# Other column cuts in the last output tile, and another queue for its second store

## The chip, the cores and the metric

The kernel runs on one core of a Trainium2 chip. The metric is the device time of one execution in microseconds; three runs of the kernel before gave a median of 223.0 us (222.99 to 223.22). One further execution was taken by the hardware profiler. Engines are named as in the profile: PE is TensorE's matmuls and PEld its weight loads, DVE is VectorE, ACT is ScalarE, POOL is GpSimd, SP is SyncE, which issues most of the DMAs. "SPq" and "ACTq" in a row stand for a DMA issued by SP or ACT.

## What is computed

The input is x, 2048 tokens of 640 columns in bf16. With xn the layer norm of x over its columns, the output is `x + s * g`:

- s is a linear attention with 32 heads of 20 columns: q, k and v come from `xn @ wqkv`; q and k go through `where(t > 0, t + 1, exp(t)) + 1e-6`; per head the sums over all tokens of k times v and of k alone are formed; q times the first is divided by q times the second, and the result goes through `wo`.
- g is `silu(relu(xn @ w1) @ w2)` with 1728 hidden columns.

```
s = _A_ref(xn, A_wqkv, A_wo)
g = _silu(_B_ref(xn, B_w1, B_w2))
return x + s * g
```

## The kernel before, in words

The tokens are cut into 16 tiles of 128. A first part of the kernel normalizes, makes k and its feature map for every tile, q for every block of 512 tokens (`pqT`) and the hidden layer (`hT`). A middle part forms the sums over the tokens, divides q by its denominator in place (`pqT`), and folds v's weights, the sums and `wo` into one matrix `wf` of 640 x 640, so that s of a tile is just `pqT` of that tile times `wf`. The last part makes the output tile by tile.

In that last part the tiles are taken in 8 pairs, `pairs[p]`; the last pair is tiles 11 and 15. For a tile, `U_main` (line 841) and `U_halves` (line 857) make the second matmul of g into two banks of PSUM, 320 columns in each; `U_silu` (lines 872 and 875) is the Silu on ACT into `g_sb`; `s_tile` (line 879) makes s and the output. `bank(p, u)` (line 834) says which two of the eight PSUM banks a tile uses; `HN` is 320 and `D` is 640.

`s_tile` for any tile but the last: ten matmuls (line 887), five for each half of 320 columns, since the sum runs over 640 rows in 5 chunks of 128; then one product on DVE, s from PSUM times g, into a buffer `tmpo` (line 909); one addition on DVE, `tmpo` plus x, into `outb` (line 894); one DMA to the output, issued by SP (line 897).

`s_tile` for the last tile, tile 15 (call on line 967, `last=True`): the columns are cut into three parts (line 885), each with five matmuls into a bank of its own: columns 0 to 319, 320 to 511 and 512 to 639. DVE makes one product for each (line 902). After the first product POOL adds x to the first part (line 906) and SP stores it; the second and third part get one addition on DVE over 320 columns (line 907) and one store, issued by SP as well. The helper `add` (line 893) holds the addition and its store.

Who waits for whom is not written by hand: a small scheduler (`Sched`) keeps, for each named piece of a buffer, its last writer and readers, and puts a wait on a semaphore ahead of an instruction where one is needed. Every engine runs its own list strictly in the order in which the program names the operations. A product of the last tile names both halves of g, `gk` (lines 891 and 904), so each waits for both Silu instructions of the tile; the second of these (line 962) works on columns 320 to 639. A DMA stands in the list of the engine that issues it, takes a semaphore of its own and counts as landed when that has reached 16. At the end SP waits for all DMAs (line 969), and a barrier over the engines closes the program (line 971).

ACT issues one DMA in the whole kernel before, a piece of w1 at the very start (line 369); all others are SP's.

Of the kernel before, what the change touches and what calls it, by code (L numbers as in the profile page):

```python
# [211 lines left out]
def bass_recurrent_scan__linear_attn_block__dense_activation_relu__prompt_kernel(  # L212
# [9 lines left out]
    Bb, S, D = A_x.shape  # L222
# [11 lines left out]
    HN = D // 2  # L234
# [11 lines left out]
    out2 = out[0]  # L246
# [17 lines left out]
    outb = reg3[:, VC * D:(VC + NOUT) * D].rearrange("p (a n) -> p a n", a=NOUT)  # L264
# [48 lines left out]
    def ps2(b, n):  # L313
        return psT[:, 512 * b:512 * (b + 2)].rearrange("p (a n) -> p a n", a=2)[:, :, 0:n]
# [7 lines left out]
    def dma(E, fn, R=(), W=(), extra=()):  # L322
        i = nds[0]
        nds[0] += 1
        return sc.dma(E, fn, i, R=R, W=W, extra=extra)

    def tok(t):
        return slice(P * t, P * (t + 1))
# [155 lines left out]
    def two(ap):  # L484
        return ap.rearrange("p (a n) -> p a n", a=2)
# [219 lines left out]
    for j in range(1, J):  # L705
# [11 lines left out]
        for n, (kind, jj, f) in enumerate(blocks):  # L717
# [4 lines left out]
            if j + 1 < J:  # L722
# [6 lines left out]
                if n in (9, 12, 14, 17):  # L729
                    t = t0 + (9, 12, 14, 17).index(n)  # L730
# [103 lines left out]
    def bank(p, u):  # L834
        return 4 * ((p + 1) % 2) + 2 * u
# [43 lines left out]
    def s_tile(p, u, b, last=False):  # L879
        t = pairs[p][u]  # L880
        os_ = so[0] % NOUT
        so[0] += 1
        i = t // 4

        parts = [(b, 0, HN), (b + 1, HN, 512), (bank(7, 0), 512, D)] if last else [(b, 0, HN), (b + 1, HN, D)]
        for pb, lo, hi in parts:
            sc.group("PE", [(lambda eng, c=c, pb=pb, lo=lo, hi=hi: eng.matmul(  # L887
                ps[pb][:, 0:hi - lo], lhsT=pqT[:, c, tok(t)], rhs=wf[:, c, lo:hi],
                start=(c == 0), stop=(c == C - 1))) for c in range(C)],
                R=[("pqT", i, c) for c in range(C)] + wfk, W=[("ps", pb)])  # L890
        gk = [("g", t, 0), ("g", t, 1)]

        def add(E, lo, hi, keys):
            sc.op(E, lambda eng: eng.tensor_tensor(out=outb[:, os_, lo:hi], in0=tmpo[:, os_, lo:hi],  # L894
                                                   in1=xre[:, t, lo:hi], op=ALU.add),
                  R=[("tmpo", os_, k) for k in keys] + [("xre", t // 4)], W=[("outb", os_, k) for k in keys])
            dma("SP", lambda eng: eng.dma_start(out2[tok(t), lo:hi], outb[:, os_, lo:hi]),
                R=[("outb", os_, k) for k in keys])

        if last:  # L900
            for k, (pb, lo, hi) in enumerate(parts):
                sc.op("DVE", lambda eng, pb=pb, lo=lo, hi=hi: eng.tensor_tensor(  # L902
                    out=tmpo[:, os_, lo:hi], in0=ps[pb][:, 0:hi - lo], in1=g_sb[:, t, lo:hi], op=ALU.mult),
                    R=[("ps", pb)] + gk, W=[("tmpo", os_, k)])
                if k == 0:
                    add("POOL", lo, hi, (0,))
            add("DVE", HN, D, (1, 2))
        else:
            sc.op("DVE", lambda eng: eng.tensor_tensor(  # L909
                out=two(tmpo[:, os_, :]), in0=ps2(b, HN), in1=two(g_sb[:, t, :]), op=ALU.mult),  # L910
                R=[("ps", b), ("ps", b + 1)] + gk, W=[("tmpo", os_, k) for k in range(3)])
            add("DVE", 0, D, (0, 1, 2))
# [31 lines left out]
    U_main(1, 1)  # L944
    U_silu(1, 1)
    s_tile(0, 0, 4)
    s_tile(0, 1, 6)
    for p in range(2, 8):
        opens = p % 2 == 1
        U_main(p, 0)  # L950
        if opens:
            U_silu(p, 0)
        s_tile(p - 1, 0, bank(p - 1, 0))
        U_main(p, 1, (0,))
        if p == 7:
            U_silu(p, 1, 0)
        s_tile(p - 1, 1, bank(p - 1, 1))
        if p == 7:
            s_tile(p, 0, bank(p - 1, 0))
        U_main(p, 1, (1,))  # L960
        if opens:
            U_silu(p, 1, 1 if p == 7 else None)
        else:
            U_halves((p, p + 1))
            U_silu(p, 0)
            U_silu(p, 1)
# [34 lines left out]
```

## Time and profile before

| what | value |
|---|---|
| median of 3 runs | 223.0 us (222.99 to 223.22) |
| the profiled execution's own time | 223.15 us |
| its span in the profile | 221.4 us |
| granted TensorE clock, mean | 0.999 |
| busy: PE, PEld, DVE, ACT, POOL (us) | 215.8, 133.9, 114.6, 86.1, 43.7 |
| stores to the output | 15 of 160 KB, 2 of 80 KB |

The span is the time from the first to the last instruction that the profile holds; the execution's own time is 1.75 us longer (223.15 less 221.4), which lies before and after. Times in rows are counted from the start of the span. A row of the timeline has the start, the duration, engine, line, operation, output and inputs with their shapes, and in brackets how long the engine was idle before and who ended that. Rows of equal instructions are merged ("x5"), and the duration is then from the first's start to the last's end. A DMA's row has the time that the issuing engine was busy with it; its landing is given apart, counted from the issue.

### The profile page before, as it was taken

Reading aid. Unit: us, or ns where it says so; the run is one execution under the profiler, and the core shown is the slowest. Engines: PE = TensorE matmul, PEld = TensorE weight load, DVE = VectorE, ACT = ScalarE, POOL = GpSimd, SP = SyncE. Lnnn points to the kernel's source line nnn. Section 1 sums busy time; section 2 is a strip of 40 time slices with the busy share of each in tenths; the row PEclk is TensorE's granted clock in tenths of the full one; section 3 lists DMA queues with packets and bytes.
Section 4 is the critical chain, followed back from the end, with each engine's and each line's share of the span. In section 5 each row is a group of like instructions: output and inputs, shape, how many; then the busy total and the mean of one; then the engine's idle time right before and its main releaser. Section 6 shows DMA issues by size and latency. Waiting matters only on the chain.

```text
span 221.4 us, 3528 instructions
## 1 busy us (share of the span) xinstructions
PE 215.8 (97%) x1463; PEld 133.9 (60%) x1474; DVE 114.6 (52%) x193; ACT 86.1 (39%) x138; POOL 43.7 (20%) x66
## 2 busy tenths in 40 slices
PE   7999999999999999999999999999999999999994
PEld 2865554455545554444467778767767776776672
DVE  2687845889687999996710006603322222314063
ACT  2368665567656656555322114641021102110300
POOL 4053101259222998700000000000000000000001
PEclk9999999999999999999999999999999999999999
DMA  6899581211012105800059969369110101000002
GB/s 190 242 357 250 131 234 41 59 30 33 0 30 59 33 0 104 170 12 3 0 178 365 272 178 353 93 201 322 62 59 3 61 30 33 30 31 33 30 30 89
DMA packets 28156, 24.51 MB, mean 111 GB/s; under 512 B 11796, under 2 KB 27500, under 8 KB 28140
## 3 DMA queue, kind: packets, MB, share of 16 engines
q1 hardware_dynamic: 27484, 23.79, 36.7%
q10 hardware_dynamic: 656, 0.49, 0.8%
q8 instruction: 11, 0.18, 0.4%
q14 instruction: 5, 0.04, 0.1%
HBM read 15.75 MB, written 5.24 MB: 95 GB/s over the span
## 4 chain that ended last, share of the span: by engine, by line
PE 95%; DVE 1%; DMA 1%; issue 0%; ACT 0%
PE psT L841 26%; PE psT L555 25%; PE psT L472 10%; PE psT L786 10%; PE psT L540 10%; PE psT L887 10%; DMA reg<-in_A_x_dram 1%; PE psT L857 1%; PE psT L577 1%; PE psT L797 1%; PE psT L808 1%; PE psT L645 1%; PE psT L450 1%; DVE reg L902 0%; DVE stats L392 0%
## 5 line engine op out<-in xcount | busy, mean ns | idle before, releaser
L555 PE MATMUL psT<-reg 128*128 128x512 bf16 (+1 forms) x295 | 59.8, 346 | 0.7 <-issue 0.2
L841 PE MATMUL psT<-reg,hT 128*128 128x320 bf16 x416 | 60.1, 299 | 0.0
L841 PEld LDWEIGHTS psT<-reg,hT 128*128 128x128 bf16 x416 | 40.4, 98 | 16.4 <-issue 1.1
L555 PEld LDWEIGHTS psT<-reg 128*128 128x128 bf16 x305 | 27.3, 98 | 26.8 <-issue 0.4
L909 DVE TENSOR_TENSOR reg<-psT,reg 128x640 bf16<-128x640 f32 x15 | 12.4, 825 | 54.0 <-PE psT L887 53.9
L562 ACT ACTIVATE hT<-psT 128x512 bf16<-128x512 f32 x52 | 30.9, 598 | 18.2 <-PE psT L555 18.1
L875 ACT ACTIVATE reg<-psT 128x640 bf16<-128x640 f32 (+1 forms) x13 | 8.4, 661 | 44.3 <-PE psT L841 24.9
L894 POOL TENSOR_TENSOR reg<-reg 128x320 bf16<-128x320 bf16 x1 | 0.8, 788 | 124.6 <-DVE reg L902 124.6
L540 PE MATMUL psT<-reg 128*128 128x512 bf16 x99 | 24.6, 379 | 0.1
L472 PE MATMUL psT<-reg 128*128 128x320 bf16 x160 | 24.2, 299 | 0.0
L481 POOL TENSOR_TENSOR zacc<-zacc,reg 128x640 f32<-128x640 f32 x16 | 23.7, 1484 | 1.9 <-DVE reg L515 1.0
L887 PE MATMUL psT<-reg,pqT 128*128 128x320 bf16 (+2 forms) x165 | 24.0, 295 | 0.0
L786 PE MATMUL psT<-reg 128*128 128x320 bf16 x160 | 21.9, 299 | 0.0
L472 PEld LDWEIGHTS psT<-reg 128*128 128x128 bf16 x160 | 15.6, 98 | 8.2
L887 PEld LDWEIGHTS psT<-reg,pqT 128*128 128x128 bf16 x165 | 15.9, 98 | 6.0
L786 PEld LDWEIGHTS psT<-reg 128*128 128x128 bf16 x160 | 15.7, 98 | 6.2
L550 DVE SCALAR_TENSOR_TENSOR pqT<-er 128x512 bf16<-128x512 bf16 x20 | 17.1, 853 | 0.7
L540 PEld LDWEIGHTS psT<-reg 128*128 128x128 bf16 x100 | 9.7, 98 | 11.7 <-DVE er L548 0.6
L392 DVE BATCH_NORM_STATS2 stats<-reg 128x6 f32<-128x320 bf16 x32 | 14.0, 478 | 3.4 <-DMA reg<-in_A_x_dram 3.4
L547 ACT ACTIVATE er<-psT 128x512 bf16<-128x512 f32 x20 | 12.0, 598 | 8.9 <-PE psT L540 8.1
L548 DVE TENSOR_SCALAR er<-psT 128x512 bf16<-128x512 f32 x20 | 13.6, 679 | 3.1 <-ACT er L547 3.1
L515 DVE TENSOR_TENSOR reg<-ek 128x640 bf16<-128x640 bf16 x16 | 13.5, 843 | 1.5 <-ACT ek L506 1.0
(66 smaller groups left out, 134.6 us busy)
## 6 DMA issues: line engine op xcount, KB each, us to landing
reg<-in_A_x_dram SPq DMA_DIRECT2D x16, 160.0 KB, 4.1
rscr<-rden SPq DMA_DIRECT2D x4, 640.0 KB, 10.7
reg<-rscr SPq DMA_DIRECT2D x5, 512.0 KB, 6.1
reg<-in_A_x_dram SPq DMA_DIRECT2D x4, 640.0 KB, 6.2
out_dram<-reg SPq DMA_DIRECT2D x15, 160.0 KB, 1.8
reg<-in_A_wqkv_dram SPq DMA_DIRECT2D x2, 800.0 KB, 6.9
reg<-in_B_w_dram SPq DMA_DIRECT2D x1, 1120.0 KB, 5.9
reg<-in_B_w_dram SPq DMA_DIRECT2D x1, 1040.0 KB, 7.6
```

The lines of the kernel that those rows point to most:

```text
L392: sc.op("DVE", lambda eng, a=a: eng.bn_stats(stats[:, t, a, :], xv[:, HN * a:HN * (a + 1)]), R=[("xin", t % XR)], W=[("stats", t, a)])
L472: fns.append(lambda eng, a=a, k=k: eng.matmul(ps[b + a][:, 0:HN], lhsT=xnT[:, k, tok(t)], rhs=wqk[:, k, D + HN * a:D + HN * (a + 1)], star ...
L481: sc.op("POOL", lambda eng: eng.tensor_tensor(out=zacc[:, :], in0=zacc[:, :], in1=pk[:, t, :], op=ALU.add), R=[("zacc",), ("pk", t)], W=[( ...
L515: sc.op("DVE", lambda eng: eng.tensor_tensor(out=pk[:, t, :], in0=e_, in1=r_, op=ALU.add), R=[("ek_e", es), ("ek_r", es)], W=[("pk", t)])
L540: sc.group("PE", [(lambda eng, k=k: eng.matmul(ps[b], lhsT=wqk[:, k, P * f:P * (f + 1)], rhs=rhs(k), start=(k == 0), stop=(k == C - 1))) f ...
L548: sc.op("DVE", lambda eng: eng.tensor_scalar(out=r_, in0=ps[b], scalar1=0.0, scalar2=1e-6, op0=ALU.max, op1=ALU.add), R=[("ps", b), ("er_e ...
L550: sc.op("DVE", lambda eng: eng.scalar_tensor_tensor(out=pqT[:, f, schunk(j)], in0=e_, scalar=1.0, in1=r_, op0=ALU.min, op1=ALU.add), R=[(" ...
L555: return sc.group("PE", [(lambda eng, k=k: eng.matmul(ps[b][:, lo:hi], lhsT=w1_sb[:, k, P * f:P * (f + 1)], rhs=xnT[:, k, 512 * j + lo:512 ...
L562: sc.op("ACT", lambda eng: eng.activation(out=hT[:, f, schunk(j)], in_=ps[b], func=ACTF.Relu), R=[("ps", b)], W=[("hT", j, f)])
L786: fns.append(lambda eng, t=t, a=a: eng.matmul(ps[b + a][:, 0:HN], lhsT=xn[:, t, P * k:P * (k + 1)], rhs=pk[:, t, HN * a:HN * (a + 1)], sta ...
L841: sc.group("PE", [(lambda eng, f=f, n=n: eng.matmul(ps[b + n][:, 0:HN], lhsT=hT[:, f, tok(t)], rhs=w2_sb[:, f, HN * n:HN * (n + 1)], start ...
L887: sc.group("PE", [(lambda eng, c=c, pb=pb, lo=lo, hi=hi: eng.matmul(ps[pb][:, 0:hi - lo], lhsT=pqT[:, c, tok(t)], rhs=wf[:, c, lo:hi], sta ...
```

## The change

The last tile is cut into 256, 192 and 192 columns in place of 320, 192 and 128. POOL's addition and the first store then cover 256 columns (64 KB) in place of 320 (80 KB), DVE's addition and the second store 384 columns (96 KB) in place of 320. And the second store is issued by ACT in place of SP: `add` gets a parameter for the issuing engine.

```diff
-        parts = [(b, 0, HN), (b + 1, HN, 512), (bank(7, 0), 512, D)] if last else [(b, 0, HN), (b + 1, HN, D)]
+        parts = [(b, 0, 256), (b + 1, 256, 448), (bank(7, 0), 448, D)] if last else [(b, 0, HN), (b + 1, HN, D)]
...
-        def add(E, lo, hi, keys):
+        def add(E, lo, hi, keys, Q="SP"):
...
-            dma("SP", lambda eng: eng.dma_start(out2[tok(t), lo:hi], outb[:, os_, lo:hi]),
+            dma(Q, lambda eng: eng.dma_start(out2[tok(t), lo:hi], outb[:, os_, lo:hi]),
                 R=[("outb", os_, k) for k in keys])
...
-            add("DVE", HN, D, (1, 2))
+            add("DVE", 256, D, (1, 2), "ACT")
```

## The prediction

> **What bounds the kernel now.** I read the page first, then the chain of work that ended last, then the timeline of the last 5 us, and then single rows for the durations.
>
> ```profile
> span 221.4 us, 3528 instructions
> PE 215.8 (97%) x1463; PEld 133.9 (60%) x1474; DVE 114.6 (52%) x193; ACT 86.1 (39%) x138; POOL 43.7 (20%) x66
> PE 95%; DVE 1%; DMA 1%; issue 0%; ACT 0%
> ```
>
> PE is the bound nearly everywhere: 97% busy, 95% of the chain. The change touches no matmul but those of the last tile, so only what lies behind the last other matmul can move. The chain's end, in order of time (start, duration, what):
>
> ```profile
> 215.00 1.77 PE psT L841 x13
> 216.76 0.69 PE psT L887 x5
> 217.45 0.02 issue
> 217.48 0.99 DVE reg L902 x3
> 218.47 0.02 issue
> 218.49 0.52 DVE reg L894
> ```
>
> The reader is to see that PE hands over at 217.45, with the first part of the last tile, and that the rest is DVE: three products, then one addition, done at 218.49 + 0.52 = 219.01. The view stops there, as the rest is DMA. The same stretch in the timeline:
>
> ```profile
> 216.46 1.49 PEld L887 LDWEIGHTS psT<-reg,pqT 128*128 128x128 bf16 x15
> 216.60 1.53 PE L887 MATMUL psT<-reg,pqT 128*128 128x320 bf16 x15
> 216.80 0.44 ACT L875 ACTIVATE reg<-psT 128x320 bf16<-128x320 f32 x1 [4.05 <-PE psT L841]
> 218.05 0.79 POOL L894 TENSOR_TENSOR reg<-reg 128x320 bf16<-128x320 bf16 x1 [124.64 <-DVE reg L902]
> 218.86 0.33 SPq L897 DMA_DIRECT2D out_dram<-reg  x1
> 219.24 0.43 SPq L897 DMA_DIRECT2D out_dram<-reg  x1
> ```
>
> PE's 15 matmuls end at 216.60 + 1.53 = 218.13. POOL's addition ends at 218.84 and SP issues the first store at 218.86. The second store could go at 219.01, when its addition is done, but SP is busy with the first until 219.19 and issues at 219.24. So 0.23 us of the end is a queue. How long the data then takes, by the stretches of the DMA engines (length, five engines, clock, DMA share, GB/s) and the landing of the second store:
>
> ```profile
> 219.60:220.00 0.40, 0.00 (x0) 0.00 (x0) 0.00 (x0) 0.00 (x0) 0.00 (x0) 1.00 0.64 200
> 220.00:220.15 0.15, 0.00 (x0) 0.00 (x0) 0.00 (x0) 0.00 (x0) 0.00 (x0) 1.00 0.06 13
> 220.15:220.50 0.35, 0.00 (x0) 0.00 (x0) 0.00 (x0) 0.00 (x0) 0.00 (x0) 1.00 0.73 231
> 220.60:221.40 0.80, 0.00 (x0) 0.00 (x0) 0.00 (x0) 0.00 (x0) 0.00 (x0) 0.72 0.00 0
> out_dram<-reg SPq DMA_DIRECT2D x1, 80.0 KB, 1.7
> ```
>
> Two bursts with a gap between: the first store's data moves about 0.8 us after its issue, the second's about 0.9 us after its own, and the engines don't queue it behind the first. It lands at 219.24 + 1.7 = 220.94, and the span ends 0.5 us later, at 221.4, with SP's wait and the closing barrier. **The last microseconds are one chain**: PE, DVE's last product, DVE's addition, an issue, a landing, the barrier. What shortens one link shortens the kernel by as much.
>
> **The change, step by step.** Durations come from these groups (last number: mean ns of one):
>
> ```profile
> L887 PE MATMUL psT<-reg,pqT 128*128 128x320 bf16 x5 | 0.8, 299 | 0.0
> L887 PE MATMUL psT<-reg,pqT 128*128 128x192 bf16 x5 | 0.6, 246 | 0.0
> L887 PE MATMUL psT<-reg,pqT 128*128 128x128 bf16 x5 | 0.4, 219 | 0.0
> L902 DVE TENSOR_TENSOR reg<-psT,reg 128x320 bf16<-128x320 f32 x1 | 0.5, 491 | 1.1 <-PE psT L887 1.1
> L902 DVE TENSOR_TENSOR reg<-psT,reg 128x192 bf16<-128x192 f32 x1 | 0.4, 357 | 0.0
> L902 DVE TENSOR_TENSOR reg<-psT,reg 128x128 bf16<-128x128 f32 x1 | 0.3, 291 | 0.0
> L894 DVE TENSOR_TENSOR reg<-reg 128x320 bf16<-128x320 bf16 x1 | 0.5, 522 | 0.0
> L894 DVE TENSOR_TENSOR reg<-reg 128x640 bf16<-128x640 bf16 x3 | 1.5, 493 | 0.1
> ```
>
> *Matmuls.* Still 15, still 640 columns five times over, so PE still ends at 218.13. A column costs (299 - 219) / 192 = 0.417 ns, so the first part, five matmuls with 64 columns fewer, is done 5 x 64 x 0.417 = 133 ns earlier, at 217.32. The weight loads are as many as before, 15 in 1.49 us, and kept up even with the 128-column matmuls; that costs nothing.
>
> *Products.* By the three rows 64 columns cost DVE 66 to 67 ns; 256 columns take 424 ns. The first starts at 217.48 - 0.13 = 217.35 and ends at 217.77. It also waits for ACT's Silu, done at 216.80 + 0.44 = 217.24; that cover shrinks from 0.24 to 0.11 us and costs nothing while it lasts. The second, even if it only starts then, is done by 217.77 + 0.36 = 218.13. So the third starts when PE is done, as before: the chain's row ends at 217.48 + 0.99 = 218.47, less 0.29 for the old third product is 218.18. It now has 192 columns: 357 in place of 291 ns, **0.07 us later**, done at 218.54.
>
> *DVE's addition.* This is the step to look at twice. Before, 320 columns took 522 ns, but 640 columns of the same line take 493 in every other tile. Half the work for more time: something holds it. Beside it runs POOL's addition, until 218.84. The other place where the two engines meet shows the same:
>
> ```profile
> 52.17 1.40 POOL L481 TENSOR_TENSOR zacc<-zacc,reg 128x640 f32<-128x640 f32 x1
> 52.30 1.61 DVE L515 TENSOR_TENSOR reg<-ek 128x640 bf16<-128x640 bf16 x1
> L515 DVE TENSOR_TENSOR reg<-ek x16: 491/493/1612, 18.5 to 87.1; 128x640 bf16<-128x640 bf16 x16
> ```
>
> The same 640-column addition takes 491 ns mostly and 1.61 us when POOL started first: it ends at 53.91, 0.34 after POOL's end at 53.57. And 219.01 is 0.17 after POOL's 218.84. 640 columns need 0.34 and 320 need 0.17 behind POOL, so about 0.53 ns a column is the work itself, and 493 - 640 x 0.52 = 158 ns is the start, which passes while DVE waits. A free addition of n columns takes 158 + 0.523 n: 384 columns take 359 ns. Free it starts at 218.54 + 0.02 (the chain's gap) = 218.56 and ends at 218.92. If POOL still runs, the end is POOL's end + 0.21, so it costs something only if POOL ends after 218.71.
>
> *POOL's addition.* Before, it started at 218.05, 0.08 after the first product's end at 217.97; now at 217.85. No row has 256 columns. In proportion to columns it takes 788 x 256 / 320 = 630 ns; with nothing saved it takes 788. It ends between 218.48 and 218.64, in both cases before 218.71. I take 630. The hold is gone, and DVE's addition ends at 218.92 in place of 219.01: **0.09 to 0.10 earlier**, though it has 64 columns more and starts 0.07 later.
>
> *Issues.* The first store follows POOL by 0.02: at 218.50 to 218.66, and SP is free 0.33 + 0.05 later, at 218.88 to 219.04. With the second store in its list SP would issue it at 218.94 to 219.04. ACT has nothing behind its last Silu (done 217.24) but this store, so no other work waits behind it; at SP's reaction of 0.02 it issues at 218.94, so its own queue is worth 0 to 0.10. Against 219.24 before that is **0.30 earlier**, of which the addition's end is 0.10 and the queue the rest; the recut alone would have brought 0.20 to 0.30 of it, since it also frees SP earlier.
>
> The Trainium skill ("DMA: Bandwidth & Descriptors", section "Issuing engines are not separate DMA queues") says that DMAs issued by different engines end up on the same 16 DMA engines and that issuing from several saves only the sequencer's time for the issue. By that rule the queue's part of this change is worth 0.00 to 0.10 us once the cuts are changed, which is what the two issue times above give; the trace before has no store from ACT to test it.
>
> *Landing.* ACT's only DMA so far, and all stores of the last part:
>
> ```profile
> reg<-in_B_w_dram ACTq DMA_DIRECT2D x1, 480.0 KB, 4.4
> L369 ACTq DMA_DIRECT2D reg<-in_B_w_dram x1: 454/454/454, 0.8 to 0.8; - x1
> L335 SPq DMA_DIRECT2D reg<-in_A_x_dram x1: 402/402/402, 0.8 to 0.8; - x1
> out_dram<-reg SPq DMA_DIRECT2D x15, 160.0 KB, 1.8
> DMA to landing us min/median/max: 1.6/1.6/1.7
> DMA to landing us min/median/max: 1.6/1.8/3.2
> SPq L897 <- DVE reg L894: 63.6, 15, 7.1
> ```
>
> The two rows of landings are those of the two small stores (80 KB: 1.6 alone, 1.7 behind the other) and of all 17. ACT's issue of 454 ns was that of a transfer six times as large as 80 KB; at the same moment SP needed 402 for its first one. 160 KB landed after 1.8. 96 KB alone should take 1.65. Unknown is what a store from ACT takes: as low as 1.5, should a queue of its own help, as high as 1.9 with a dearer issue (454 against 332 adds 0.12) and some meeting with the first store, whose data, issued at 218.5 or 218.66, moves until about 219.8. I take 1.65, nearest to the two 80 KB rows. It lands at 220.59, **0.05 less to land** than 1.7. The first store lands at the latest at 218.66 + 1.7 = 220.36 and is not last. Behind the landing SP waits and the barrier closes as before, 0.5 us.
>
> *Sum.* 0.30 + 0.05 = 0.35 earlier in the landing; with the rounding of the 1.7 (two digits) I take 0.3. The span becomes 221.1, the profiled execution's 223.15 becomes 222.85, and the median, which is 0.15 under that execution, 223.0 - 0.3 = **222.7 us**. That is 0.13% less. About 0.2%, 0.45 us, is what a measurement of this kernel can tell from no change, so the forecast is a gain within it.
>
> **The rivals.** *A larger gain.* It needs 0.15 us more than the sum. The only links with that much room are the landing and the issue: a landing of 1.5 from a queue of its own gives 0.45 and 222.55, and if 0.05 to 0.1 more comes off at the closing barrier, 222.45. For it speaks that the second store's issue before, right behind another, cost 0.43 against 0.33, and a clean issue may bring the whole 0.10 and not 0.05; against it the gap between the bursts, which shows that the data did not queue. *The old hold remains.* If POOL's shorter addition still ends after 218.71 (it would have to take over 0.86, longer than the larger one), DVE ends up to 0.1 later, and 0.2 is left: 222.8. Little speaks for it. *Slower.* The store from ACT lands late: ACT's queue carried nothing for 218 us, and the store that nobody follows is the one for which everybody waits. Stores of this part landed after 3.2 us at the worst, 1.4 above their median; the forecast turns into a loss when the landing takes over 1.65 + 0.3 = 1.95, and into one beyond 0.2% from 2.4. At 3.2 the time would be 223.0 - 0.3 + 1.55 = 224.2. For it: ACT's one DMA landed after 4.4 us, but that was 480 KB among other loads. Against it: SP too waited 63.6 us in 15 times before its stores, 4 us each, and the large ones still landed after 1.8 in the median. *Nothing happens at all* would need a landing that does not follow the issue; then 223.0.
>
> **How the numbers follow.** Forecast, 222.5 to 222.95 with 222.7 as its middle, the hold included: 0.64. Larger gain, under 222.55: 0.24. ACT's landing eats the gain without going beyond 0.2%, 222.95 to 223.4: 0.05. Slower beyond 0.2%: 0.07. So faster by over 0.2% has 0.24, within 0.2% has 0.69, slower by over 0.2% has 0.07. The range reaches from 222.4, the larger gain with a little spread of the runs, to 223.05, where the landing has eaten all; beyond its ends I leave some 0.08 below and 0.1 above.
>
> **What would show it.** In the profile of the changed kernel: the first product starts near 217.35; the third still near 218.18 and takes 357; DVE's addition over 384 columns takes about 360 ns and not over 500; POOL is done before it starts or soon after; the store from ACT is issued near 218.94, while SP's is issued near 218.5; it lands 1.6 to 1.7 later; the span is 221.1. An addition still over 500 ns would refute the reading of POOL's hold; a landing over 1.9 the reading of ACT's queue; a first product not earlier than 217.45 would show that the Silu or something else bounds it. A change anywhere ahead of 216.4 would mean that the recompiled program moved in a way that no step here covers.

## The result, and the profile after

The changed kernel takes 222.68 us in the median of 22 runs (222.32 to 223.08); the kernel before, run beside it, 223.08 us (222.82 to 223.45). The ratio is 0.998 with a 95% interval of 0.9974 to 0.9987, so it is faster, by 0.29 to 0.58 us. The profiled execution took 222.65 us with a span of 220.9.

The page of the profile after differs from that of before only in the span, in small shares of the chain, and in up to 0.2 us of busy time:

```profile
span 220.9 us, 3528 instructions
PE 215.6 (98%) x1463; PEld 133.8 (61%) x1474; DVE 114.6 (52%) x193; ACT 86.1 (39%) x138; POOL 43.6 (20%) x66
PE 95%; DMA 2%; issue 0%; DVE 0%; ACT 0%; SPq 0%
```

The span is 0.51 us shorter (221.425 to 220.919 in the trace), but not all of that is the change. The timeline of the end after the change, from the last tile's matmuls on, without the weight loads (start, duration, engine, line, operation):

```profile
216.42 1.53 PE L887 MATMUL psT<-reg,pqT 128*128 128x256 bf16 x15
216.62 0.44 ACT L875 ACTIVATE reg<-psT 128x320 bf16<-128x320 f32 x1 [4.05 <-PE psT L841]
217.16 1.18 DVE L902 TENSOR_TENSOR reg<-psT,reg 128x256 bf16<-128x256 f32 x3 [0.96 <-PE psT L887]
217.67 0.67 POOL L894 TENSOR_TENSOR reg<-reg 128x256 bf16<-128x256 bf16 x1 [124.43 <-DVE reg L902]
218.36 0.33 SPq L897 DMA_DIRECT2D out_dram<-reg  x1
218.38 0.36 DVE L894 TENSOR_TENSOR reg<-reg 128x384 bf16<-128x384 bf16 x1
218.77 0.36 ACTq L897 DMA_DIRECT2D out_dram<-reg  x1
```

The 15 matmuls start at 216.42; before, it was 216.60. **0.18 us of the 0.51 had been gained ahead of the last tile**, in a part that the change doesn't touch; more on that below. So the end is best measured from the start of these 15 matmuls, and all times in the following table, from the trace, are counted from there, in us:

| | before | after | earlier by |
|---|---|---|---|
| first product starts | 0.880 | 0.746 | 0.134 |
| POOL's addition ends | 2.238 | 1.917 | 0.321 |
| third product ends | 1.862 | 1.928 | -0.066 |
| DVE's addition ends | 2.418 | 2.320 | 0.098 |
| second store issued | 2.640 | 2.352 | 0.288 |
| second store landed | 4.327 | 3.999 | 0.328 |
| end of the span | 4.827 | 4.503 | 0.324 |

The last row is called the tail from here on. Read downwards, it is the sum: 0.098 from the addition, 0.190 from the queue, 0.040 from the landing (1.647 after the issue in place of 1.687), and 0.004 given back at the barrier.

### The profile page after: what moved, and what is told of

Its sections match the earlier page's. It is cut to its first block, busy times and chain, and to the rows that moved or that the text cites. A ratio compares the mean times of both kernels' runs of the same rounds, so it can differ in the third digit from the quotient of the medians.

```text
span 220.9 us, 3528 instructions
## 1 busy us (share of the span) xinstructions
PE 215.6 (98%) x1463; PEld 133.8 (61%) x1474; DVE 114.6 (52%) x193; ACT 86.1 (39%) x138; POOL 43.6 (20%) x66
## 4 chain that ended last, share of the span: by engine, by line
PE 95%; DMA 2%; issue 0%; DVE 0%; ACT 0%; SPq 0%
PE psT L841 26%; PE psT L555 25%; PE psT L887 10%; PE psT L786 10%; PE psT L472 10%; PE psT L540 10%; DMA reg<-in_A_x_dram 2%; PE psT L857 1%; PE psT L577 1%; PE psT L797 1%; PE psT L808 1%; PE psT L645 1%; PE psT L450 1%; PE psT L438 0%; ACT reg L441 0%
## 5 line engine op out<-in xcount | busy, mean ns | idle before, releaser
L894 POOL TENSOR_TENSOR reg<-reg 128x256 bf16<-128x256 bf16 x1 | 0.7, 667 | 124.4 <-DVE reg L902 124.4
```

## The experiments

Many effects are a few hundredths of a microsecond, less than the timed runs can tell apart: the kernel before against itself gave 0.9997 with an interval of 0.9989 to 1.0006, some 0.2 us to either side. In the two kernels that were profiled twice the tail repeats within 0.013 us, most of it in the closing barrier; the landing of the second store, counted from the same start, repeats within 0.005. So the tail decides, and the ratio is given beside it. Each other kernel has one profile. Code cuts are against the changed kernel where nothing else is said.

**Two controls.** The kernel before and the changed kernel, each unchanged, once more.

> The kernel before, unchanged, as a control. The profiles of before and after differ by 0.51 us in the span, of which 0.18 us is there by 12 us from the start, far ahead of the change; the rest, measured from the start of the last tile's 15 matmuls to the end of the span, is 4.82 against 4.50 us. Theory A (the early 0.18 is what one execution differs from the next): the last 15 matmuls start anywhere from 216.3 to 216.9 here too, and from there to the end it is 4.82 again. Theory B (the early shift belongs to the changed program): they start at 216.60 within 0.03. The ratio should be 1.000 within some 0.001, which shows what five rounds can tell.

> The changed kernel, unchanged, as a second control beside the last kernel on one chip. Tail 4.50 within 0.01 again; the last 15 matmuls start anywhere from 216.3 to 216.9, since what lies ahead of them differs between executions. By the tail alone it is 0.32 us under before.

| | tail | last 15 matmuls start | ratio to before (95%) |
|---|---|---|---|
| before, first profile | 4.827 | 216.60 | |
| before, again | 4.815 | 216.85 | 0.9997 (0.9989 to 1.0006) |
| after, first profile | 4.503 | 216.42 | 0.998 (0.9974 to 0.9987) |
| after, again | 4.490 | 216.40 | 0.998 (0.9971 to 0.9989) |

Theory A holds for the size: the kernel before started its last matmuls 0.25 us later the second time, more than the 0.18 in question. Over twelve profiles that start lies between 216.32 and 217.85. All of the shift is there after the first 10 us: from then on to the last tile, ACT's instructions in each of the twelve keep the same distance from those of before to within 0.02 us. The chain at the start shows two parts of it. Here are the landing of the first tile of x and, further on, an instruction of ACT: in the kernel before, in the same kernel again, and in the slowest of the twelve (the last kernel below), one fence each:

```profile
0.79 2.61 DMA reg<-in_A_x_dram
...
7.60 0.71 ACT reg L441
```

```profile
0.79 2.66 DMA reg<-in_A_x_dram
...
7.87 0.71 ACT reg L441
```

```profile
0.79 2.76 DMA reg<-in_A_x_dram
...
8.83 0.71 ACT reg L441
```

The landing is the smaller part: it comes 0.05 and 0.15 us later than in the first fence, where ACT's instruction comes 0.27 and 1.23 us later. Most of the rest is the pace of TensorE in between. The same five matmuls, in the second profile of the kernel before and in the slowest of the twelve (duration of one in ns, minimum, median and maximum, then when they start):

```profile
L450 PE MATMUL psT<-reg,onesM x5: 219/219/219, 7.1 to 7.3; 128*128 128x128 bf16 x5
```

```profile
L450 PE MATMUL psT<-reg,onesM x5: 314/314/314, 7.5 to 8.0; 128*128 128x128 bf16 x5
```

The pace changes once: in these traces, matmuls of 128 columns in a row start 0.107 us apart before it and 0.056 us apart after it. The change came 5.9 us after the start in the kernel before, 6.7 us in the same kernel again and 8.8 us in the slowest; in both profiles of the changed kernel the fast pace was there by 4.9 us.

What stays open: both profiles of the changed kernel start early, both of before late, and the differences of the medians tend to be larger than those of the tails. The fast pace came early, too, in the run below that has the cuts of before and only the queue changed, and late in two with other cuts (a first part of 384 columns, and the last kernel), so in these runs it goes neither by the cuts nor by the queue; what sets it they don't show. A small share of the early shift could still belong to the program; with starts of 216.32 to 217.85 for kernels that are all alike up to the last tile, these runs don't settle it.

**Only the cuts; both stores from SP.**

```diff
-            add("DVE", 256, D, (1, 2), "ACT")
+            add("DVE", 256, D, (1, 2), "SP")
```

> Only the cuts of 256, 192 and 192; the second store stays with SP. My theory (POOL's hold on DVE and the early first store bring the gain, the queue nearly nothing): DVE's addition takes 357 ns, SP has issued the first store by then, issues the second 2.35 us after the start of the last 15 matmuls, and from that start to the end it is 4.50 to 4.60 us (4.82 before, 4.50 with both parts). Rival (the queue of its own brings the gain): 4.70 to 4.80.

The timeline of this kernel, and the landing of its second store (KB, us):

```profile
216.32 1.53 PE L887 MATMUL psT<-reg,pqT 128*128 128x256 bf16 x15
...
218.26 0.33 SPq L897 DMA_DIRECT2D out_dram<-reg  x1
218.28 0.36 DVE L894 TENSOR_TENSOR reg<-reg 128x384 bf16<-128x384 bf16 x1
...
218.67 0.40 SPq L897 DMA_DIRECT2D out_dram<-reg  x1
```

```profile
out_dram<-reg SPq DMA_DIRECT2D x1, 96.0 KB, 1.7
```

The reader is to see that SP is done with the first store at 218.59, before the addition ends at 218.64, and issues the second 2.351 after the start of the matmuls, as early as ACT did with both parts (2.352). Tail 4.536, ratio 0.9988 (0.9980 to 0.9997). The cuts alone bring 0.291 of the 0.324; what the queue adds to them is 0.033 (0.046 by the second profile of the changed kernel), nearly all of it in the landing (1.685 against 1.647). SP's issue right behind another took 403 ns, ACT's 360; counted from the end of the issue, the 96 KB land after 1.28 and 1.29.

**Only the queue; cuts as before.**

```diff
-        parts = [(b, 0, 256), (b + 1, 256, 448), (bank(7, 0), 448, D)] if last else [(b, 0, HN), (b + 1, HN, D)]
+        parts = [(b, 0, HN), (b + 1, HN, 512), (bank(7, 0), 512, D)] if last else [(b, 0, HN), (b + 1, HN, D)]
...
-            add("DVE", 256, D, (1, 2), "ACT")
+            add("DVE", HN, D, (1, 2), "ACT")
```

> Only the second store from ACT; the cuts stay 320, 192 and 128. My theory: DVE's addition is still held by POOL and takes about 520 ns; ACT issues 0.02 after its end, 2.45 us after the start of the last 15 matmuls in place of 2.64; it lands after 1.60 to 1.65; from that start to the end 4.55 to 4.63 us. Alone, each part then brings most of the gain, and the two together less than their sum. Rival (ACT's issue or landing is dearer than SP's, and the gain came from the cuts): 4.70 to 4.85.

Its timeline:

```profile
217.82 0.79 POOL L894 TENSOR_TENSOR reg<-reg 128x320 bf16<-128x320 bf16 x1 [124.63 <-DVE reg L902]
218.27 0.52 DVE L894 TENSOR_TENSOR reg<-reg 128x320 bf16<-128x320 bf16 x1
218.64 0.33 SPq L897 DMA_DIRECT2D out_dram<-reg  x1
218.82 0.36 ACTq L897 DMA_DIRECT2D out_dram<-reg  x1
```

The addition still takes 0.52 beside POOL. ACT issues at 218.82 while SP is busy until 218.97: that is the queue saved. The landing took 1.66, a little over the expected 1.60 to 1.65. Tail 4.615, ratio 0.9987 (0.9978 to 0.9996). Alone the queue brings 0.212, alone the cuts 0.291, together 0.324: **the two remove the same wait**, SP's 0.19 us (2.640 before, 2.450 here), and the second to be applied finds little left.

**POOL's addition left out; cuts and queue as before** (code cut against the kernel before).

```diff
-                    add("POOL", lo, hi, (0,))
+                    dma("SP", lambda eng, lo=lo, hi=hi: eng.dma_start(out2[tok(t), lo:hi], tmpo[:, os_, lo:hi]),
+                        R=[("tmpo", os_, 0)])
```

> Cuts and queue as before, but POOL's addition left out: columns 0 to 319 of the last tile are stored as s times g, without x. My theory (POOL holds DVE's addition): the addition over 320 columns takes 325 ns in place of 522; the first store is issued 1.40 us after the start of the last 15 matmuls, the second 2.25, and from that start to the end it is 4.35 to 4.42 us. Rival (320 columns of this shape cost 522 ns by themselves): the second is issued 2.45 after that start, and it is 4.55 to 4.65.

The group of the addition in this kernel (busy us, mean ns, idle before):

```profile
L894 DVE TENSOR_TENSOR reg<-reg 128x320 bf16<-128x320 bf16 x1 | 0.3, 325 | 0.0
```

The same addition, at the same place (1.897 after the start of the matmuls), takes 325 ns where it took 522 with POOL beside it. The rival, that 320 columns cost that much by themselves, is out. Tail 4.325, a little under the expected 4.35 to 4.42, since the landing from an idle SP took 1.583. The ratio, 0.9991 (0.9968 to 1.0013), is too wide to say anything.

**A longer addition on POOL:** cuts of 384, 128 and 128, second store from ACT.

```diff
-        parts = [(b, 0, 256), (b + 1, 256, 448), (bank(7, 0), 448, D)] if last else [(b, 0, HN), (b + 1, HN, D)]
+        parts = [(b, 0, 384), (b + 1, 384, 512), (bank(7, 0), 512, D)] if last else [(b, 0, HN), (b + 1, HN, D)]
...
-            add("DVE", 256, D, (1, 2), "ACT")
+            add("DVE", 384, D, (1, 2), "ACT")
```

> Cuts of 384, 128 and 128 columns, second store from ACT: POOL's addition is longer, DVE's shorter (256 columns). All times from the start of the last 15 matmuls. My theory (POOL's hold: DVE's addition ends 0.012 + 0.523 ns a column after POOL's end): POOL runs from about 1.65 to 2.56 (909 ns, on the line through 667 for 256 and 788 for 320 columns), DVE's addition starts near 2.04 and ends near 2.70, so it takes about 660 ns where free it would take 292; the whole tail is 4.75 to 4.85, no better than before. Rival (no hold, or one that shares rather than stops): the addition takes 290 to 450 ns.

The two additions as groups, and the landing of the second store:

```profile
L894 POOL TENSOR_TENSOR reg<-reg 128x384 bf16<-128x384 bf16 x1 | 0.9, 909 | 124.8 <-DVE reg L902 124.8
L894 DVE TENSOR_TENSOR reg<-reg 128x256 bf16<-128x256 bf16 x1 | 0.7, 705 | 0.0
```

```profile
out_dram<-reg ACTq DMA_DIRECT2D x1, 64.0 KB, 1.7
```

The smallest of the additions on DVE is the slowest: 705 ns for 256 columns. It ends at 2.705, 0.146 after POOL's 2.559; the sum on record said near 2.70. (It starts 0.04 earlier than I had worked out, hence 705 and not 660.) The tail of 4.938 is over the expected 4.75 to 4.85: ACT's issue at 2.737 fell into SP's (2.586 to 2.918), and 64 KB then took 1.697 to land, where 64 KB took 1.559 from SP in the changed kernel and 1.595 from ACT with SP idle (next run). Without that 0.10 the tail would lie within the range. A single execution took 223.42 us.

**The queues swapped:** first store from ACT, second from SP, cuts as changed.

```diff
-                    add("POOL", lo, hi, (0,))
+                    add("POOL", lo, hi, (0,), "ACT")
...
-            add("DVE", 256, D, (1, 2), "ACT")
+            add("DVE", 256, D, (1, 2), "SP")
```

> The changed kernel with the two queues swapped: the first store (64 KB) from ACT, the second (96 KB) from SP, which then has nothing of the last tile ahead of it. Of 0.5 us more or less nothing is at stake here: my theory (issuing from a queue that has just issued costs 0.04 us, and ACT's issue of 360 ns against SP's 332 costs 0.03): SP issues at 2.35 after the start of the last 15 matmuls, in 332 ns, and it lands after 1.60 to 1.63; tail 4.46 to 4.49 against 4.50 of the change. Rival (ACT and SP are the same, and the 1.65 is the 96 KB): 4.50 to 4.52.

Its two stores in the timeline:

```profile
218.54 0.36 ACTq L897 DMA_DIRECT2D out_dram<-reg  x1
218.94 0.33 SPq L897 DMA_DIRECT2D out_dram<-reg  x1
```

Tail 4.472, ratio 0.9972 (0.9954 to 0.9990). SP's 96 KB landed after 1.618, ACT's after 1.647 in the changed kernel: an issue from ACT is dearer by 28 ns (360 against 332), and its landings come 0.03 to 0.04 later (64 KB: 1.595 against 1.559). Counted from the end of the issue, the 96 KB land after 1.29 from either engine, so the issue is all the difference that these profiles show. The gain over the change is 0.03 in the landing and 0.02 to 0.03 in the tail, by which of the two profiles of the changed kernel one takes.

**Cuts of 272, 208 and 160.**

```diff
-        parts = [(b, 0, 256), (b + 1, 256, 448), (bank(7, 0), 448, D)] if last else [(b, 0, HN), (b + 1, HN, D)]
+        parts = [(b, 0, 272), (b + 1, 272, 480), (bank(7, 0), 480, D)] if last else [(b, 0, HN), (b + 1, HN, D)]
...
-            add("DVE", 256, D, (1, 2), "ACT")
+            add("DVE", 272, D, (1, 2), "ACT")
```

> Cuts of 272, 208 and 160 columns, second store from ACT. My theory: the third product takes 324 ns in place of 357, DVE's addition (368 columns) 350 in place of 357 and is still free, since POOL (697 ns) ends near 2.00 and would hold it only to 2.20, before its own end near 2.28; all is 0.04 earlier than in the change, tail 4.46. Rival (the second product, 208 columns, is late, or POOL's hold reaches further than the sum says): 4.50 or more.

Tail 4.471: 0.02 to 0.03 under the change, where 4.46 was expected. The addition ends at 2.279 as worked out; ACT's issue at 2.311 meets the end of SP's (until 2.357) and lands after 1.655. A single execution took 222.68 us.

**The second store in two halves** of 64 partitions, from SP and ACT at once, cuts as changed.

```diff
-            dma(Q, lambda eng: eng.dma_start(out2[tok(t), lo:hi], outb[:, os_, lo:hi]),
-                R=[("outb", os_, k) for k in keys])
+            cuts = [("SP", 0, 64), ("ACT", 64, 128)] if Q == "ACT" else [(Q, 0, 128)]
+            for q, r0, r1 in cuts:
+                dma(q, lambda eng, r0=r0, r1=r1: eng.dma_start(
+                    out2[P * t + r0:P * t + r1, lo:hi], outb[r0:r1, os_, lo:hi]),
+                    R=[("outb", os_, k) for k in keys])
```

> The changed kernel with the second store cut by partitions into two of 48 KB, one from SP and one from ACT, issued at the same time. My theory (what follows the issue is a fixed way, not the amount of data): each lands 1.55 to 1.70 after its issue, and the tail is 4.45 to 4.60, no gain that can be measured. Rival (the landing goes with the data per issue): landing 1.45 or less and a tail under 4.35.

The two halves in the timeline, and their landings:

```profile
218.76 0.55 SPq L899 DMA_DIRECT2D out_dram<-reg  x1
218.76 0.56 ACTq L899 DMA_DIRECT2D out_dram<-reg  x1
```

```profile
out_dram<-reg SPq DMA_DIRECT2D x1, 48.0 KB, 1.9
out_dram<-reg ACTq DMA_DIRECT2D x1, 48.0 KB, 2.2
```

Both theories missed. Half the data each, and the landing takes 1.93 and 2.20 in place of 1.65; both issues take over half again as long. Tail 5.046, worse than before the change; a single execution took 223.21 us. Two things are new in this run: the two issues begin at the same moment, and each covers 64 rows in place of 128. The second may be the reason for the long issues: the kernel before has two DMAs of 64 rows of 1280 bytes, issued by SP one behind the other, the first behind a load of 960 KB, with no DMA issued by another engine near them (duration in ns):

```profile
L764 SPq DMA_DIRECT2D reg<-in_B_w_dram x2: 579/583/587, 112.9 to 113.5; - x2
```

SP's issues of 128 such rows right behind one another took 416 to 432 ns at the start of the same kernel. A store of 64 rows from one engine alone was not run, so how much of the loss is the rows and how much the meeting of the two isn't shown.

**What the runs point to:** cuts of 256, 224 and 160, first store from ACT, second from SP, so that ACT's issue is just over when SP's begins.

```diff
-        parts = [(b, 0, 256), (b + 1, 256, 448), (bank(7, 0), 448, D)] if last else [(b, 0, HN), (b + 1, HN, D)]
+        parts = [(b, 0, 256), (b + 1, 256, 480), (bank(7, 0), 480, D)] if last else [(b, 0, HN), (b + 1, HN, D)]
...
-                    add("POOL", lo, hi, (0,))
+                    add("POOL", lo, hi, (0,), "ACT")
...
-            add("DVE", 256, D, (1, 2), "ACT")
+            add("DVE", 256, D, (1, 2), "SP")
```

> Cuts of 256, 224 and 160 columns, the first store from ACT and the second from SP: what the runs so far point to. The third product takes 324 ns in place of 357, DVE's addition still covers 384 columns and ends 2.29 after the start of the last 15 matmuls, and ACT's issue (1.95 to 2.31) is over when SP's begins at 2.32. My theory: tail 4.43 to 4.45, against 4.50 of the change and 4.82 of before; 0.37 to 0.39 us under before. Rival (the two issues meet, or the second product of 224 columns makes the third late): tail 4.50 or more.

The end in its timeline:

```profile
219.78 0.36 DVE L894 TENSOR_TENSOR reg<-reg 128x384 bf16<-128x384 bf16 x1
219.80 0.36 ACTq L897 DMA_DIRECT2D out_dram<-reg  x1
220.17 0.33 SPq L897 DMA_DIRECT2D out_dram<-reg  x1
```

Tail 4.449, the shortest of the full kernels, 0.378 under before and 0.04 to 0.05 under the change; median 222.57 us, ratio 0.9976 (0.9961 to 0.9991). The profiled execution was the slowest of its twelve, 224.06 us, with 1.25 us lost in the first 10 us. That it beats the change rests on the tail; beside the change on the same chip (0.998) the timed runs can't tell the two apart.

## Why the prediction was right

The forecast, 222.7 us as a gain within the bound of 0.2%, came out at 222.68, and step by step for the reasons given. That the two numbers are so close is in part luck: the forecast took 0.3 off a base of 223.0, while the kernel before measured 223.08 beside the changed one and the medians differ by 0.40.

- *Matmuls and products.* The first product was to start 0.13 earlier and did (0.134); the third was to stay and end 0.07 later, and did (0.066).
- *POOL's hold on DVE's addition* was the step on which the gain from the cuts stood. With a shorter addition on POOL, with none, and with a longer one, DVE's time went to 357, 325 and 705 ns, and where POOL still ran, DVE ended 0.146 (256 columns) and 0.181 (320, only the queue changed) after it. The Trainium skill ("SBUF — State Buffer", section "Who interferes with whom") says that a VectorE instruction with two SBUF inputs contends with a GpSimd instruction that reads SBUF, since its second input comes through a read interface that the two share, and calls the shared ports an exclusive lock; the 522 and 705 ns beside POOL and the 325 without it agree. DVE's third product, which has one input in PSUM, ran beside POOL as well and was not held: 291 ns with POOL, 292 without.
- *POOL's addition* took 667 ns, within the bounds of 630 and 788 but not the 630 that I took: a column costs (909 - 667) / 128 = 1.89 ns, and some 183 ns don't scale. It ends well before it could hold, so nothing hung on it.
- *The queue* was to be worth 0 to 0.10 once the cuts are changed; it was 0.033. The issue came at 2.351 with SP and 2.352 with ACT; ACT's was 0.043 shorter and its landing 0.038. The rule of the Trainium skill ("DMA: Bandwidth & Descriptors", section "Issuing engines are not separate DMA queues"), that issuing from several engines saves only the sequencer's time for the issue, agrees with these numbers.
- *Landing.* 1.65 was taken and 1.647 measured. That it fits to the hundredth is luck: 1.65 was taken for 96 KB alone, with the price of ACT's issue unknown; SP alone took 1.618, and ACT's issue added 0.03. ACT's 360 ns was nearer to SP's 332 than to the 454 of its one large transfer.
- *The rivals.* A larger gain needed a faster landing from a queue of its own; in the profile there is none. The medians differ by 0.40, more than the tail's 0.32; whether the rest is the spread of the start or something of the program stays open. The last sign of being wrong, a change ahead of 216.4, was too strict: the last 15 matmuls did start 0.18 earlier, but in the unchanged kernel they moved by 0.25 from one profile to the next. POOL's old hold did not remain. ACT's late landing, the slower side, did not come: no store from ACT took over 1.70 as long as no other issue began at the same moment.

What the sum had lost: rounding its 0.35 to 0.3. Unrounded, with two digits more in the landing before (1.687), it is 0.34, and the profile shows 0.324: the issue is 0.288 earlier in place of 0.30, the landing 0.040 shorter, and the barrier gives 0.004 back.

## What to carry to other kernels

Where a kernel ends in a chain of evacuation, store and barrier, walk that chain link by link, and ask of each instruction whether it takes what its shape costs elsewhere in the same trace: an addition that needed more for 320 columns than for 640 pointed to the first 0.1 us of the gain, and a store that was ready but not issued to the other 0.2. Two edits against the same wait don't add up, and the second engine's DMA queue helps only while the first is still issuing; better to let the first finish earlier. Below the spread of whole runs, compare stretches that start at the last common instruction, and have a control of the unchanged kernel.

## What the runs showed of the hardware that I had not expected

A store from ACT lands later when it is issued soon after SP's. Alone, or 0.41 us after SP's began, it took 360 ns to issue and 1.60 (64 KB) to 1.65 us (96 KB) to land. Issued 0.15 us after SP's began, 64 KB took 1.70; 0.19 us after, 80 KB took 1.66; at 0.29 us nothing is left to see (92 KB, 1.655). The issues themselves stayed at 332 and 360 ns all the while. The first packet of ACT's data moved 0.86 us after its issue began where the issues were 0.41 apart, but 0.89 and 0.96 us after it where they were 0.19 and 0.15 apart. So the two stores' data began 0.24 and 0.28 us apart, more than their issues, and 0.27 us apart with the two issues of 64 rows that began 5 ns apart: as if one store had to get through some step before the other. The Trainium skill ("Perfetto Trace Analysis", section "DMA Instruction — HWDGE (DVE, Sync)") has the engines that issue such DMAs share one descriptor generator, locked for exclusive use; that fits the spacing of the data, while the unchanged 332 and 360 ns show no wait for a lock in the issue. Such a mechanism was not tried further.

Behind POOL, DVE's blocked addition ends 0.146, 0.181 and 0.347 us after POOL's with 256, 320 and 640 columns (the last at line 515, behind POOL's line 481). It needs only its columns' time, 0.52 ns each, with 12 ns; the 158 ns that any free one has at its start pass during the wait.
